# A decode kernel's down weights: twelve rows per partition by one load in halves, and 16 partitions of 16 rows by four short loads

## The chip, the cores and the metric

The kernel runs on one core of a Trainium2 chip. The metric is device time in microseconds (us) for one execution. Several executions are timed; a profile is taken from one more. The profile's span goes from the first to the last instruction of that execution, and the execution's own time is a little longer than its span.

## The reference

Two parts are computed from small activations (8 rows of 512) and large weights and caches, and then combined. The window W is 2048 positions.

```
xn = layernorm(x)                                  # [8, 1, 512]
q  = xn @ wq                                       # 32 heads of 128
k, v = the last W positions of the caches          # 8 KV heads, each serves 4 query heads
o  = softmax(q k^T * 128**-0.5) v
s  = o @ wo                                        # [8, 1, 512]

h  = sigmoid(xn @ w_gate) * (xn @ w_up)            # [8, 1, 1792]
g  = silu(h @ w_down)                              # [8, 1, 512]

out = x + s * g
```

All inputs are bf16. w_down has 1792 rows of 512 numbers, 1 KB each. K and V of the window are 64 MiB together; all weights are about 13 MiB.

## The kernel before

**Tiles and slots.** Everything large is loaded by SP's DMA queue (`q0`, nc.sync) into nine slots of 16 KB per partition (pool `slots`, list `empty`, line 85). A wish for a load is put on the list `todo`; `pump()` (line 87) issues wishes in their order as long as a slot is free, and `free()` (line 92) gives a slot back and pumps again. So the order of the loads is the order in which they are wished for, lines 171 to 192: gate weights, up weights, down weights, the short loads ("sides") among the query weights, then K tiles and, three behind them, V tiles of each batch and half, then the output weights `wo` in four pieces of 16, 10, 4 and 2 rows per partition.

**How SP waits.** Each load raises one of eight DMA semaphores in turn; a load waits until the load eight places before it has landed. It also waits for the engine that must have read the old contents of its slot, for K and V tiles PE. The first load of all, x, goes through ACT's queue and takes the first semaphore.

**A load's engines.** A load of 128 partitions is worked on by all 16 DMA engines of the core, each of which has its own list of packets. The short loads have 5, 3 or 9 partitions.

**The down weights.** 1792 rows are 14 for each of 128 partitions; they are cut in three. `want_down` (line 143) loads the first 1408 rows as 11 consecutive rows for each of 128 partitions (tile `wd_sb`). The remaining 384 rows go into a tile `side` (lines 122 to 141): 240 rows as 15 rows on 16 partitions by two loads of five and two of three partitions (`LOW`, `SF`), and 144 rows as 4 rows on 36 partitions from partition 32 on by four loads of nine (`MID`, `SM`, `M_AT`). Each of these loads takes every fourth partition. The first 32 partitions of the tile are zeroed by POOL first (line 126), because some of them stay unfilled and are read as zero weights.

**What is done with them.** h is made from gate and up products (lines 273 to 306). It must be turned so that its 1792 numbers lie on partitions like the rows of w_down. For the first 1408 numbers PE transposes strided views of `h_bf` directly. For the side rows POOL first copies h into `h_side` in the order of the side partitions (lines 309 to 323; zeroed on line 249), and PE transposes that. DVE and ACT copy the turned h to `hT_sb` (lines 331 to 333). After the query products (lines 347 to 362), 26 products with `wd_sb` and `side` accumulate `d_ps` (lines 363 to 375). The gate value g is finished on lines 395 to 401.

**The rest.** For each batch PE transposes K tiles (line 456; DVE copies them out on line 461), multiplies them with q (line 474), ACT makes exponentials (line 494), PE turns those (line 563) and multiplies with V (line 584). At the end PE multiplies with `wo` (line 706) as its four pieces land, DVE combines and four small transfers write the output (lines 717 to 724).

Of the kernel before, what the change touches and what calls it, by code (L numbers as in the profile page):

```python
# [10 lines left out]
def kernel(  # L11
# [13 lines left out]
    nc = tc.nc  # L25
    P = 128
    B, _, D = A_x.shape
# [4 lines left out]
    F = B_w_gate.shape[1]  # L32
    KT = D // P
# [14 lines left out]
    bf16 = mybir.dt.bfloat16  # L48
# [12 lines left out]
    work = ctx.enter_context(tc.tile_pool(name="work", bufs=1))  # L61
# [17 lines left out]
    q0, q1 = nc.sync, nc.scalar  # L79
    k_tiles = {}  # L80
    v_tiles = {}
    weights = {}
# [10 lines left out]
        empty.append(int(t[1][4:]))  # L93
        pump()

    def want_rows(name, w, per, r0, r1, step=None):
        def f(tag):
            t = slots.tile([P, r1 - r0, w.shape[1]], bf16, name=name, tag=tag)
            for a in range(r0, r1, step or r1 - r0):
                z = a + (step or r1 - r0)  # L100
                q0.dma_start(
                    out=t[:, a - r0 : z - r0, :],
                    in_=w.rearrange("(p r) n -> p r n", r=per)[:, a:z, :],
                )
            rows_of[(name, r0)] = (t, tag)
            for r in range(r0, r1):
                weights[(name, r)] = t[:, r - r0, :]

        todo.append((True, f))

    LOW, SF = (5, 5, 3, 3), 15
    MID, SM = 9, 4
    SP = 4 * max(LOW)
    M_AT = 32
    MP = 4 * MID
    MT = 11
    m0 = MT * P
    m1 = m0 + SF * sum(LOW)
    assert m1 + SM * MP == F
    side = {}  # L120

    def want_side(w, q, at, count, rows, base, of):
        def f(tag=None):
            if tag:
                t = slots.tile([P, SF, w.shape[1]], bf16, name="side", tag=tag)
                nc.gpsimd.memzero(t[:M_AT])  # L126
                side["t"] = t
                rows_of[("side", 0)] = (t, tag)
                for r in range(SF):
                    weights[("wd_sb", MT + r)] = t[: M_AT + MP if r < SM else SP, r]  # L130
            q0.dma_start(  # L131
                out=side["t"][at + q : at + q + 4 * (count - 1) + 1 : 4, :rows].rearrange(
                    "p s n -> p (s n)"
                ),
                in_=w[base : base + of * count * rows, :].rearrange(
                    "(p q s) n -> q p (s n)", q=of, s=rows
                )[q % of],
            )

        todo.append((not side, f))  # L140
        side["asked"] = True

    def want_down(w):
        def f(tag):
            t = slots.tile([P, MT, w.shape[1]], bf16, name="wd_sb", tag=tag)
            q0.dma_start(
                out=t[:].rearrange("p t n -> p (t n)"),
                in_=w[: MT * P, :].rearrange("(p t) n -> p (t n)", t=MT),
            )
            rows_of[("wd_sb", 0)] = (t, tag)  # L150
            for r in range(MT):
                weights[("wd_sb", r)] = t[:, r, :]

        todo.append((True, f))
# [13 lines left out]

    RT = 32
    Z = 32  # L170
    want_rows("wg_sb", B_w_gate, KT, 0, KT, 2)
    want_rows("wu_sb", B_w_up, KT, 0, KT, 2)
    want_down(B_w_down)
    sides = []
    for q in range(4):
        sides.append((q, 0, LOW[q], SF, m0 + q // 2 * 2 * LOW[0] * SF, 2))
        sides.append((q, M_AT, MID, SM, m1, 4))
    for x in sides[:2]:
        want_side(B_w_down, *x)
    for i in range(2):  # L180
        want_rows("wq_sb", A_wq, KT, 2 * i, 2 * i + 2)
        for x in sides[2 + 3 * i : 5 + 3 * i]:
            want_side(B_w_down, *x)
    order = [(b, i) for b in range(B) for i in range(NQ)]
    AHEAD = 3
    for n in range(len(order) + AHEAD):
# [4 lines left out]
    for t0, t1 in ((0, 16), (16, 26), (26, 30), (30, RT)):  # L191
# [15 lines left out]
        out=perm[:].rearrange("k (l p) -> k l p", l=G),  # L207
        in_=ident[:].rearrange("k (p l) -> k l p", l=G),
# [11 lines left out]
        out=rstd[:], in_=mv[:, 1:2], func=AF.Sqrt, bias=eps_t[:], scale=1.0  # L220
# [4 lines left out]
        out=xn_bf[:],  # L225
# [8 lines left out]
    for kt in range(KT):  # L234
        nc.tensor.transpose(  # L235
            out=xnT_ps[:, kt, :],
            in_=xn_bf[:].rearrange("b (p kt) -> b kt p", kt=KT)[:, kt, :],
# [5 lines left out]

    hT_sb = work.tile([P, MT + SF, Z], bf16, name="hT_sb")
    nc.gpsimd.memzero(hT_sb[:])  # L245
    oP_sb = work.tile([P, RT, Z], bf16, name="oP_sb")
    nc.gpsimd.memzero(oP_sb[:])
    h_side = work.tile([B, SF, M_AT + MP], bf16, name="h_side")
    nc.gpsimd.memzero(h_side[:])

    NB = D // P

# [10 lines left out]
    with nc.allow_low_precision(reason="zeros and a one"):  # L263
        nc.vector.reduce_sum(
            out=band[:], in_=ident[:].rearrange("k (q t) -> k q t", t=RT), axis=AX.X
        )
        nc.vector.reduce_sum(
            out=pick[:], in_=ident[:].rearrange("k (q t) -> k t q", t=RT), axis=AX.X
# [21 lines left out]
    h_bf = ktpool.tile([P, CU * P], bf16, name="h_bf", tag="kT")  # L290
    for k in range(F // FC):
        u_ps = ps_t.tile([B, FC], f32, name="u_ps", tag="t")
        for kt in range(KT):
# [8 lines left out]
            out=h_bf[:B, k * FC : (k + 1) * FC],  # L302
# [3 lines left out]
        )  # L306
    free(rows_of[("wu_sb", 0)])
    hT_ps = ps_m.tile([P, MT + SF, B], bf16, name="hT_ps", tag="m")
    for h in range(2):
        c = LOW[2 * h]  # L310
        at = m0 + h * 2 * LOW[0] * SF
        nc.gpsimd.tensor_copy(
            out=h_side[:, :, : 4 * c].rearrange("b t (e q) -> b t e q", q=4)[
                :, :, :, 2 * h : 2 * h + 2
            ],
            in_=h_bf[:B, at : at + 2 * c * SF].rearrange(
                "b (e q t) -> b t e q", q=2, t=SF
            ),
        )
    nc.gpsimd.tensor_copy(  # L320
        out=h_side[:, :SM, M_AT:],
        in_=h_bf[:B, m1:F].rearrange("b (p t) -> b t p", t=SM),
    )
    cuts = [h_bf[:B, :m0].rearrange("b (p t) -> b t p", t=MT)[:, t] for t in range(MT)]
    rows = [P] * MT + [M_AT + MP] * SM + [SP] * (SF - SM)
    cuts += [h_side[:, t, : rows[MT + t]] for t in range(SF)]
    for t, x in enumerate(cuts):
        nc.tensor.transpose(
            out=hT_ps[: rows[t], t, :], in_=x, identity=ident[:B, :B]
        )  # L330
    nc.vector.tensor_copy(out=hT_sb[:, :MT, :B], in_=hT_ps[:, :MT])
    for k, t0, t1 in ((M_AT + MP, MT, MT + SM), (SP, MT + SM, MT + SF)):
        nc.scalar.copy(out=hT_sb[:k, t0:t1, :B], in_=hT_ps[:k, t0:t1])

    def fold(out_ps, src, start, stop):
        for j in range(NB):
# [38 lines left out]
    for e in range(2):  # L375
# [3 lines left out]
        for r in range(rep):  # L379
            nc.tensor.transpose(  # L380
                out=qT_ps[:, r].rearrange("p g z -> p (g z)"),
                in_=q_bf[:, r * Dh : (r + 1) * Dh],
# [3 lines left out]
            out=qm_sb[:, :, G * e : G * (e + 1), M0 : M0 + rep].rearrange(  # L386
                "p b g r -> p r g b"
            ),
            in_=qT_ps[:, :, :, :B],
# [14 lines left out]
    for j in range(NB):  # L404
# [15 lines left out]
        out=turn_rows[:].rearrange("k (x l r) -> k x l r", x=NU, l=G),  # L420
        in_=ident[:].rearrange("k (l x r) -> k x l r", x=NU, l=G),
    )
    sel_e = consts.tile([P, 2, Hq], f32, name="sel_e")
    for e in range(2):
        nc.vector.reduce_sum(
            out=sel_e[:, e, :].rearrange("k (i h) -> k i h", i=NQ),
            in_=ident_f[:].rearrange(
                "k (i m e h) -> k e i h m", i=NQ, m=NJ // 2, e=2
            )[:, e],
# [290 lines left out]
    for j in range(NB):  # L720
        (q0, q1)[j % 2].dma_start(
            out=out.flatten_outer_dims()[:, j * P : (j + 1) * P],
            in_=y_bf[Z * j : Z * j + B, :],
# [31 lines left out]
```

## Time and profile before

| what | us |
|---|---|
| median of 3 runs (199.06 to 199.09) | 199.06 |
| the profiled execution | 199.33 |
| its span | 197.5 |
| PE busy | 157.4 |
| DVE busy | 125.4 |
| ACT busy | 40.7 |
| POOL busy | 11.0 |

The mean granted clock of PE over the span is 0.965 of full speed. The span holds 4796 instructions. DMA moved 81.32 MB, 412 GB/s over the span. Busy time is summed over the span for each engine; the engines run side by side, so the rows do not add up to the span. An engine's share says little by itself: what a change is worth is read where it acts, from what is waited for there.

### The profile page before, as it was taken

To read this page: it belongs to the slowest core of one execution; us is meant where nothing else is said; L and a number is where in the kernel's file an instruction comes from. 1 tells how busy PE (TensorE), PEld (TensorE's weight loads), DVE (VectorE), ACT (ScalarE), POOL (GpSimd) and SP (SyncE) were. 2 spreads that over 40 slices of the span, in tenths; PEclk is the share of its full clock that TensorE was granted. 3 is DMA by queue.
4 is the path that set the end of the run, shared out by engine and by line. 5 is a ranking of instruction groups with operands and counts; after the bars stand their busy time and mean duration, and the time that the engine had idled before them with its cause. 6 is when DMAs were issued, how large, how long until landed. Compare 5 with 4: busy or idle time off the path is not lost.

```text
span 197.5 us, 4796 instructions
## 1 busy us (share of the span) xinstructions
PE 157.4 (80%) x2112; PEld 103.1 (52%) x2112; DVE 125.4 (63%) x245; ACT 40.7 (21%) x95; POOL 11.0 (6%) x22
## 2 busy tenths in 40 slices
PE   0089559999788898799979987999799979976733
PEld 0034325776664565466545654566466556655531
DVE  4623106999797696679666965796669658935201
ACT  0522022006306001600160016001600160071000
POOL 8910200000000000000000000000000000000000
PEclk9999859999999999999999999999999999999975
DMA  6999999999999999999999999999999999999980
GB/s 205 424 440 435 431 434 435 425 425 431 423 425 425 438 428 435 431 425 428 422 433 431 435 425 433 428 418 428 428 438 431 428 428 431 428 423 425 428 366 21
DMA packets 6396, 81.32 MB, mean 412 GB/s; under 512 B 812, under 2 KB 820, under 8 KB 1624
## 3 DMA queue, kind: packets, MB, share of 16 engines
q1 hardware_dynamic: 6328, 81.01, 96.6%
q8 instruction: 16, 0.26, 0.5%
q10 hardware_dynamic: 48, 0.01, 0.0%
q14 instruction: 4, 0.03, 0.0%
HBM read 81.01 MB, written 0.01 MB: 410 GB/s over the span
## 4 chain that ended last, share of the span: by engine, by line
DMA 73%; PE 22%; POOL 3%; SPq 0%; issue 0%; DVE 0%; POOLq 0%
DMA v_sb<-in_A_v_cache_dram 46%; DMA wo_sb<-in_A_wo_dram 14%; PE kT_ps L456 11%; DMA wq_sb<-in_A_wq_dram 7%; DMA k_sb<-in_A_k_cache_dram 6%; PE o_ps L584 4%; PE s_ps L474 3%; POOL side L126 2%; PE m_ps L614 1%; PE fin_ps L706 1%; PE pT_ps L563 1%; SPq L131 0%; POOL perm L206 0%; POOL hT_sb L245 0%; DVE prod L717 0%
## 5 line engine op out<-in xcount | busy, mean ns | idle before, releaser
L461 DVE COPY kT_sb<-kT_ps 128x1024 bf16<-128x1024 bf16 x128 | 84.2, 683 | 28.9 <-PE kT_ps L456 25.0
L456 PE MATMUL kT_ps<-perm,k_sb 128*128 128x128 bf16 x1024 | 72.6, 220 | 3.7 <-DMA k_sb<-in_A_k_cache_dram 3.7
L456 PEld LDWEIGHTS <-k_sb 128*128 128x128 bf16 x1024 | 58.8, 98 | 26.1 <-issue 16.8
L584 PE MATMUL o_ps<-v_sb,pT_sb 128*32 128x256 bf16 (+1 forms) x352 | 36.5, 327 | 9.0 <-DMA v_sb<-in_A_v_cache_dram 7.6
L474 PE MATMUL s_ps<-kT_sb,qm_sb 128*32 128x512 bf16 x256 | 25.6, 389 | 1.3 <-DVE kT_sb L461 1.1
L494 ACT ACTIVATE p_buf<-s_ps,st 32x512 bf16<-32x512 f32 x32 | 21.7, 679 | 15.4 <-DVE st L487 15.1
L584 PEld LDWEIGHTS <-pT_sb 128*32 128x32 bf16 (+1 forms) x352 | 12.3, 101 | 21.7 <-issue 19.7
L604 ACT ACTIVATE o_sb<-o_ps,fac 128x512 f32<-128x512 f32 (+1 forms) x8 | 4.9, 608 | 60.9 <-PE o_ps L584 60.9
L568 DVE COPY pT_sb<-pT_ps 128x1024 bf16<-128x1024 bf16 x16 | 10.8, 676 | 1.8 <-PE pT_ps L563 1.8
L474 PEld LDWEIGHTS <-qm_sb 128*32 128x32 bf16 x256 | 7.0, 93 | 8.0 <-issue 1.3
L563 PE MATMUL pT_ps<-turn_rows,p_buf 128*128 128x128 bf16 x128 | 10.7, 227 | 0.0
L563 PEld LDWEIGHTS <-p_buf 128*128 128x128 bf16 x128 | 9.4, 149 | 0.2 <-issue 0.2
L521 ACT ACTIVATE w_row<-w 1x128 f32<-1x128 f32 x8 | 2.5, 309 | 30.6 <-DVE w L514 30.6
L235 PE MATMUL xnT_ps<-ident,xn_bf 8*128 8x8 bf16 x4 | 0.3, 176 | 10.6 <-DVE xn_bf L224 10.6
L385 DVE COPY qm_sb<-qT_ps 128x128 bf16<-128x128 bf16 x2 | 1.4, 881 | 8.7 <-PE qT_ps L380 8.7
L301 DVE TENSOR_TENSOR h_bf<-sig,u_ps 8x448 bf16<-8x448 f32 x4 | 2.4, 608 | 6.6 <-PE u_ps L294 6.1
L278 PE MATMUL g_ps<-wg_sb,xnT_sb 128*8 128x448 bf16 x16 | 5.7, 544 | 0.3 <-DVE xnT_sb L242 0.3
L494 ACT ACTIVATION_READ_ACCUMULATOR p_buf<-s_ps,st 32x1 f32 x32 | 5.9, 184 | 0.0
L706 PE MATMUL fin_ps<-wo_sb,oP_sb 128*32 128x128 bf16 x128 | 3.3, 263 | 3.1 <-DMA wo_sb<-in_A_wo_dram 3.1
L487 DVE TENSOR_REDUCE st<-s_ps 128x1 f32<-128x512 f32 x8 | 5.4, 681 | 0.5 <-PE s_ps L474 0.5
L235 PEld LDWEIGHTS <-xn_bf 8*128 8x128 bf16 x4 | 0.2, 117 | 10.6 <-DVE xn_bf L224 10.6
L352 PE MATMUL q_ps<-wq_sb,xnT_sb 128*32 128x512 bf16 x32 | 3.1, 526 | 3.2 <-DMA wq_sb<-in_A_wq_dram 3.2
(88 smaller groups left out, 92.0 us busy)
## 6 DMA issues: line engine op xcount, KB each, us to landing
k_sb<-in_A_k_cache_dram SPq DMA_DIRECT2D x16, 2048.0 KB
v_sb<-in_A_v_cache_dram SPq DMA_DIRECT2D x16, 2048.0 KB
wq_sb<-in_A_wq_dram SPq DMA_DIRECT2D x2, 2048.0 KB
wo_sb<-in_A_wo_dram SPq DMA_DIRECT2D x1, 2048.0 KB
wg_sb<-in_B_w_gate_dram SPq DMA_DIRECT2D x2, 896.0 KB
wu_sb<-in_B_w_up_dram SPq DMA_DIRECT2D x2, 896.0 KB
wd_sb<-in_B_w_down_dram SPq DMA_DIRECT2D x1, 1408.0 KB
wo_sb<-in_A_wo_dram SPq DMA_DIRECT2D x1, 1280.0 KB
```

Of the source, the lines that this page charges most:

```text
L126: nc.gpsimd.memzero(t[:M_AT])
L278: nc.tensor.matmul(g_ps[:], lhsT=xnT_sb[:, kt, :B], rhs=weights[("wg_sb", kt)][:, k * FC : (k + 1) * FC], start=(kt == 0), stop=(kt == KT ...
L456: nc.tensor.transpose(out=kT_ps[:, c, :], in_=k_sb[:, j * CU + h * CH + c, :], identity=perm[:],)
L461: nc.vector.tensor_copy(out=kT[(b, u)][:, h * CH : (h + 1) * CH, :], in_=kT_ps[:])
L474: nc.tensor.matmul(s_ps[b][NR * l : NR * (l + 1), :], lhsT=qm_sb[:, b, i * G + l, o : o + Z], rhs=t[:, :, PG * l : PG * (l + 1)], start=(u ...
L487: nc.vector.tensor_reduce(out=st[b][:], in_=s_ps[b][:], axis=AX.X, op=ALU.max, negate=True)
L494: nc.scalar.activation(out=p_buf[b % 2][rows, :, l, :], in_=s[rows, :].rearrange("k (c p) -> k p c", p=PG), func=AF.Exp, bias=st[b][rows, ...
L563: nc.tensor.transpose(out=pT_ps[:, c, :], in_=p_buf[b % 2][:, :, :, h * CH + c].rearrange("k p l -> k (p l)"), identity=turn_rows[:],)
L568: nc.vector.tensor_copy(out=pT[b][:, h * CH : (h + 1) * CH, :], in_=pT_ps[:])
L584: nc.tensor.matmul(o_ps[r] if b < WIDE else o_ps[r, 0:2], lhsT=pT[b][:, c, r], rhs=x, start=(c == 0), stop=(c == CU - 1), tile_position=(0 ...
L604: nc.scalar.activation(out=o[:, :n], in_=o_ps[:, :n], func=AF.Copy, scale=fac.pop(b)[:])
L706: nc.tensor.matmul(fin_ps[Z * j : Z * (j + 1), :], lhsT=oP_sb[:, t, :], rhs=weights[("wo_sb", t)][:, j * P : (j + 1) * P], start=(t == 0), ...
```

## The change

The 1792 rows are cut in two instead of three. The large load takes 12 rows for each of 128 partitions (1536 rows). The remaining 256 rows go to 16 partitions, 16 rows each, by two loads of five partitions and two of three; each takes every second partition. There are no loads of nine partitions. All 16 partitions of the side tile are filled, so nothing is zeroed, and the side rows of h lie in an order that PE can transpose from `h_bf` directly, so `h_side`, its zeroing and POOL's three copies go. There are 28 instead of 26 transposes and products.

Some loads are issued as two halves of 64 partitions each: the first of the two gate loads, the large down load, and both query loads. The gate and up loads are two each of two rows per partition, as before. The number of loads on SP's queue ahead of the first K tile is 15 before and after. All four short loads now stand ahead of the last query load: two of five partitions between the large load and the first query load, two of three between the query loads.

```diff
+    def halves(parts, out, in_):
+        n = P // parts
+        for a in range(0, P, n):
+            q0.dma_start(out=out[a : a + n], in_=in_[a : a + n])
+
-    def want_rows(name, w, per, r0, r1, step=None):
+    def want_rows(name, w, per, r0, r1, parts=(1,)):
         def f(tag):
             t = slots.tile([P, r1 - r0, w.shape[1]], bf16, name=name, tag=tag)
-            for a in range(r0, r1, step or r1 - r0):
-                z = a + (step or r1 - r0)
-                q0.dma_start(
-                    out=t[:, a - r0 : z - r0, :],
-                    in_=w.rearrange("(p r) n -> p r n", r=per)[:, a:z, :],
+            n = (r1 - r0) // len(parts)
+            for a, k in zip(range(r0, r1, n), parts):
+                halves(
+                    k,
+                    t[:, a - r0 : a - r0 + n, :],
+                    w.rearrange("(p r) n -> p r n", r=per)[:, a : a + n, :],
                 )
...
-    LOW, SF = (5, 5, 3, 3), 15
-    MID, SM = 9, 4
-    SP = 4 * max(LOW)
-    M_AT = 32
-    MP = 4 * MID
-    MT = 11
+    LOW, SF = (5, 5, 3, 3), 16
+    SP = sum(LOW)
+    MT = 12
     m0 = MT * P
-    m1 = m0 + SF * sum(LOW)
-    assert m1 + SM * MP == F
+    assert m0 + SF * SP == F
     side = {}
 
-    def want_side(w, q, at, count, rows, base, of):
+    def want_side(w, p0, q, count):
         def f(tag=None):
             if tag:
                 t = slots.tile([P, SF, w.shape[1]], bf16, name="side", tag=tag)
-                nc.gpsimd.memzero(t[:M_AT])
...
+            at = m0 + p0 * SF
             q0.dma_start(
-                out=side["t"][at + q : at + q + 4 * (count - 1) + 1 : 4, :rows].rearrange(
-                    "p s n -> p (s n)"
-                ),
-                in_=w[base : base + of * count * rows, :].rearrange(
-                    "(p q s) n -> q p (s n)", q=of, s=rows
-                )[q % of],
+                out=side["t"][p0 + q : p0 + 2 * count : 2].rearrange("p s n -> p (s n)"),
+                in_=w[at : at + 2 * count * SF, :].rearrange(
+                    "(p q s) n -> q p (s n)", q=2, s=SF
+                )[q],
             )
...
             t = slots.tile([P, MT, w.shape[1]], bf16, name="wd_sb", tag=tag)
-            q0.dma_start(
-                out=t[:].rearrange("p t n -> p (t n)"),
-                in_=w[: MT * P, :].rearrange("(p t) n -> p (t n)", t=MT),
+            halves(
+                2,
+                t[:].rearrange("p t n -> p (t n)"),
+                w[: MT * P, :].rearrange("(p t) n -> p (t n)", t=MT),
             )
...
-    want_rows("wg_sb", B_w_gate, KT, 0, KT, 2)
-    want_rows("wu_sb", B_w_up, KT, 0, KT, 2)
+    want_rows("wg_sb", B_w_gate, KT, 0, KT, (2, 1))
+    want_rows("wu_sb", B_w_up, KT, 0, KT, (1, 1))
     want_down(B_w_down)
...
     for i in range(2):
-        want_rows("wq_sb", A_wq, KT, 2 * i, 2 * i + 2)
-        for x in sides[2 + 3 * i : 5 + 3 * i]:
-            want_side(B_w_down, *x)
+        for q in range(2):
+            want_side(B_w_down, i * 2 * LOW[0], q, LOW[2 * i])
+        want_rows("wq_sb", A_wq, KT, 2 * i, 2 * i + 2, (2,))
...
-    h_side = work.tile([B, SF, M_AT + MP], bf16, name="h_side")
-    nc.gpsimd.memzero(h_side[:])
...
-    rows = [P] * MT + [M_AT + MP] * SM + [SP] * (SF - SM)
-    cuts += [h_side[:, t, : rows[MT + t]] for t in range(SF)]
+    cuts += [h_bf[:B, m0:F].rearrange("b (p t) -> b t p", t=SF)[:, t] for t in range(SF)]
+    rows = [P] * MT + [SP] * SF
...
-    for k, t0, t1 in ((M_AT + MP, MT, MT + SM), (SP, MT + SM, MT + SF)):
-        nc.scalar.copy(out=hT_sb[:k, t0:t1, :B], in_=hT_ps[:k, t0:t1])
+    nc.scalar.copy(out=hT_sb[:SP, MT:, :B], in_=hT_ps[:SP, MT:])
```

More of the change, by code (lines that the diff above doesn't have):

```diff
@@ L129, in f @@
                 for r in range(SF):
-                    weights[("wd_sb", MT + r)] = t[: M_AT + MP if r < SM else SP, r]
+                    weights[("wd_sb", MT + r)] = t[:SP, r]
+            at = m0 + p0 * SF
             q0.dma_start(
-                out=side["t"][at + q : at + q + 4 * (count - 1) + 1 : 4, :rows].rearrange(
-                    "p s n -> p (s n)"
-                ),
-                in_=w[base : base + of * count * rows, :].rearrange(
-                    "(p q s) n -> q p (s n)", q=of, s=rows
-                )[q % of],
+                out=side["t"][p0 + q : p0 + 2 * count : 2].rearrange("p s n -> p (s n)"),
+                in_=w[at : at + 2 * count * SF, :].rearrange(
+                    "(p q s) n -> q p (s n)", q=2, s=SF
+                )[q],
             )
@@ L170 @@
     Z = 32
-    want_rows("wg_sb", B_w_gate, KT, 0, KT, 2)
-    want_rows("wu_sb", B_w_up, KT, 0, KT, 2)
+    want_rows("wg_sb", B_w_gate, KT, 0, KT, (2, 1))
+    want_rows("wu_sb", B_w_up, KT, 0, KT, (1, 1))
     want_down(B_w_down)
[L174 to L178, printed above, removed]
-        want_side(B_w_down, *x)
     for i in range(2):
-        want_rows("wq_sb", A_wq, KT, 2 * i, 2 * i + 2)
-        for x in sides[2 + 3 * i : 5 + 3 * i]:
-            want_side(B_w_down, *x)
+        for q in range(2):
+            want_side(B_w_down, i * 2 * LOW[0], q, LOW[2 * i])
+        want_rows("wq_sb", A_wq, KT, 2 * i, 2 * i + 2, (2,))
     order = [(b, i) for b in range(B) for i in range(NQ)]
@@ L308 @@
     hT_ps = ps_m.tile([P, MT + SF, B], bf16, name="hT_ps", tag="m")
[L309 to L323, printed above, removed]
     cuts = [h_bf[:B, :m0].rearrange("b (p t) -> b t p", t=MT)[:, t] for t in range(MT)]
-    rows = [P] * MT + [M_AT + MP] * SM + [SP] * (SF - SM)
-    cuts += [h_side[:, t, : rows[MT + t]] for t in range(SF)]
+    cuts += [h_bf[:B, m0:F].rearrange("b (p t) -> b t p", t=SF)[:, t] for t in range(SF)]
+    rows = [P] * MT + [SP] * SF
     for t, x in enumerate(cuts):
```

## The prediction

> **What bounds the kernel now.** I read the page's slices first (its second part), then the DMA queues, the chain that ended last, and then windows of the span's two ends.
>
> ```profile
> DMA  6999999999999999999999999999999999999980
> GB/s 205 424 440 435 431 434 435 425 425 431 423 425 425 438 428 435 431 425 428 422 433 431 435 425 433 428 418 428 428 438 431 428 428 431 428 423 425 428 366 21
> ...
> q1 hardware_dynamic: 6328, 81.01, 96.6%
> q8 instruction: 16, 0.26, 0.5%
> ...
> DMA 73%; PE 22%; POOL 3%; SPq 0%; issue 0%; DVE 0%; POOLq 0%
> ```
>
> The sixteen DMA engines are busy in every slice but the two ends, at about 430 GB/s. All weights and caches, 81.01 MB, go through SP's one queue. The chain is DMA for 73%, and its PE pieces lie beside transfers that were running anyway. So the end comes when the queue is empty, plus a tail.
>
> ```profile
> 189.50:190.00 0.50, 0.39 (x28) 0.24 (x17) 0.00 (x0) 0.00 (x0) 0.00 (x0) 1.00 1.11 467
> 190.00:190.50 0.50, 0.00 (x0) 0.00 (x0) 0.00 (x0) 0.00 (x0) 0.00 (x0) 0.77 0.82 344
> 190.50:191.00 0.50, 0.00 (x0) 0.00 (x0) 0.00 (x0) 0.00 (x0) 0.00 (x0) 0.50 0.71 295
> 191.00:191.50 0.50, 0.00 (x0) 0.00 (x0) 0.00 (x0) 0.00 (x0) 0.00 (x0) 0.50 0.80 324
> 191.50:192.00 0.50, 0.14 (x8) 0.14 (x11) 0.00 (x0) 0.00 (x0) 0.00 (x0) 0.50 0.92 360
> 192.00:192.50 0.50, 0.50 (x28) 0.50 (x24) 0.00 (x0) 0.00 (x0) 0.00 (x0) 0.50 0.67 262
> 192.50:193.00 0.50, 0.50 (x24) 0.42 (x16) 0.00 (x0) 0.00 (x0) 0.00 (x0) 0.50 0.45 172
> 193.00:193.50 0.50, 0.50 (x23) 0.40 (x16) 0.00 (x0) 0.00 (x0) 0.00 (x0) 0.50 0.07 25
> ```
>
> Columns: window, length, busy time of PE, PEld, DVE, ACT and POOL, PE's clock, DMA share, GB/s. The rate does not drop at once; it thins out over 3.5 us. The engines do not finish together, and the output waits for the last one. Each engine works through a list of its own, so what counts is not the sum of bytes but the list of the slowest engine. This is the view on which the forecast rests.
>
> The trace's records of single packets and of completion counts give those lists. A load of all partitions is counted complete by 16 engines, one of nine partitions by nine, one of five by five, one of three by three. A 16384-byte packet takes 611 ns and the next one on its engine starts 607 ns after it, so 27.0 GB/s for each engine. The first K load, right behind the weights, completes on its sixteen engines at 29.56 to 29.98 us (eight), 30.28 to 30.52 (three), 31.06 and 31.14, and 32.39 to 32.45 (three): those that carried the short loads are late in that order. From there I followed each engine packet by packet. The sixteen instruction blocks of q8 come to eight engines in turn, at 31.8 us, 41.1 and so on, and each delays its engine by about 1.42 us (881 ns for itself, 1158 instead of 611 for the next packet, less 14 of overlap and the 4 by which packets overlap). None comes to the five engines that carry the five-row and three-row loads, which is why those can carry more.
>
> **The change, part by part.** *Bytes per engine.* The large load gives every engine 8 rows of 11 KB now (88 KB) and 8 of 12 KB then (96). The short loads give now: to the first three engines 4 x 15 + 4 x 4 = 76 KB, the next two 2 x 15 + 16 = 46, the next four 16, the last seven nothing. Then: 4 x 16 = 64, 2 x 16 = 32, nothing, nothing. Sums 164, 134, 104, 88 before; 160, 128, 96, 96 after. At 607 ns for 16 KB this is -0.15, -0.23, -0.30 and +0.30 us. The last data of the slowest engine of each group ends, by my tracking, at 193.22, 193.04, 193.36 and 193.02. After: 193.07, 192.81, 193.06 and 193.32. The last one ends at 193.32 in place of 193.36: **-0.04 us**. The gain of one group is the loss of another. (Of the four engines with 16 KB more, one can't be told apart from the last seven; if the 193.02 is its, the next is 192.95 and the sum is -0.11.)
>
> *Halves of 64 partitions.* One gate load, the large load and both query loads are halved. The count of loads on SP stays 15: four halves more, four short loads fewer. All sixteen engines serve a half too, with four packets each where a whole load has eight. No load of before goes to 64 partitions. Lower bound: nothing. The nearest row is the short load of five: five engines write 15360 bytes each to partitions of one 20-partition stretch and take 573 ns, 26.8 GB/s, the rate of any other. Upper bound, if half the partitions took only half the rate: the halves hold 0.92 + 1.57 + 4.19 = 6.68 MB, 15.5 us at 432 GB/s, so 15.5 us more. I take nothing, because the row with the fewest partitions shows no loss, though its partitions lie four apart; the upper bound is the first rival.
>
> *Start.* Before:
>
> ```profile
> 1.00:2.00 1.00, 0.00 (x0) 0.00 (x0) 0.00 (x0) 0.00 (x0) 0.90 (x4) 1.00 0.62 79
> 2.00:3.00 1.00, 0.00 (x0) 0.00 (x0) 0.26 (x1) 0.00 (x0) 1.00 (x1) 1.00 0.63 173
> 3.00:4.00 1.00, 0.00 (x0) 0.00 (x0) 1.00 (x1) 0.00 (x0) 1.00 (x1) 1.00 0.91 366
> 4.00:5.00 1.00, 0.00 (x0) 0.00 (x0) 1.00 (x1) 0.00 (x0) 1.00 (x1) 1.00 0.98 409
> ```
>
> The first weight packet starts at 1.77 us. By 5.0 us 432 GB/s would have moved 1395 KB, and 1027 KB were moved: 0.85 us lost. A first load of half the size may gain some of it, 0.85 at most, or lose as much where its four packets run out before the next half is described. Each first packet took 560 to 1412 ns where later ones of 7168 bytes take 272, whatever load stood behind it, so I take 0, with 0.2 either way.
>
> *SP and POOL.*
>
> ```profile
> L131 SPq DMA_DIRECT2D side<-in_B_w_down_dram x8: 690/744/864, 5.1 to 16.9; - x8
> L126 POOL MEMSET side<- x1: 3287/3287/3287, 1.8 to 1.8; 32x3840 uint32 x1
> ```
> ```profile
> SPq L131 <- POOL hT_sb L245: 2.2, 1, 2.2
> ```
>
> The zeroing of the side tile (3.29 us of POOL) and SP's wait for POOL go, with POOL's second zeroing (0.51) and three copies (0.73 + 0.30). Worth nothing: the load in front of the wait, the large one, lands only at 15.35 us, 10 us after SP goes on, so the queue was full. Behind SP's wait stood the short loads and the query loads, and nobody waits for those before 22 us. Four short issues of 744 ns become four of about 413 (a gate load's), 1.3 us less on SP. SP's later waits are for the eighth load before; every place of that chain moves earlier or stays, since the number of loads is the same.
>
> *PE.* Two transposes and two products more (26 to 28 tiles), 0.11 us for each product (1.64 us by 15). What moves is the second query half: all short loads now lie ahead of it. The first three engines have 160 KB of down weights in front of it, not 88 + 53 = 141, so it lands 0.7 us later than 26.67. From there PE's row of work runs 5.5 us to 32.2; then it would end near 33.1, and the first K load, landed by 32.3, waits 0.6 us longer than the 0.04 of before. The cover is PE's own waiting: it sat 1.24 us at 81.09 for a V load, and the page gives PE 7.6 us of waits for V and 3.7 for K. Without that cover 0.6 us would be lost. SP's K and V issues that follow wait for PE to free a slot, but run some 33 us ahead of their landing at 42.57 us, so 0.6 us starves no engine. ACT's one copy for two, and DVE's 96 columns for 88, lie beside the wait for the query load.
>
> *Tail.* Unchanged: from the last completion, 193.69 us, to the end of the span at 197.5.
>
> Sum: span 197.5 - 0.04; the profiled execution is 199.33, so 199.29. The median of the runs is 199.06, 0.27 below the profiled one: 199.02. Several engines of three groups now stand within 0.3 us of the last, and a new start reorders them by up to 0.2, which raises the largest more than it lowers it: I add 0.1 and say **199.1 us**.
>
> **Rivals.** *Halves are slow (slower).* If two engines that write into the same half of the partitions share a way in, the eight halves (6.68 MB) run at down to half rate, and everything behind them in the queue is late by up to 15.5 us: 206 to 214.6. For it: no load of before has this form, and before's short loads are placed four partitions apart, so they can't show the crowding. Against it: 573 ns for five engines in 20 partitions. It decides from a loss of 2.6% in those 15.5 us, 0.4 us. [...]
>
> *An instruction block falls on a loaded engine (slower).* The last of the sixteen blocks starts at 191.889 us on an engine whose data ended at 191.887. PE has eight more instructions, and eight engines take the blocks in turn. If the block, or one more, comes to an engine that still has data, that engine ends 1.42 us later; on one that ends at 193.3 the end moves by up to 1.4: 199.5 to 200.5, deciding from 0.4. Against it: that engine's data now end 0.30 us earlier, at 191.59, and the block's time follows PE, which follows the loads.
>
> *A better start (faster).* The 0.85 us lost before 5 us come back in part with a smaller first load: 198.2 to 198.6. Against it: the slow first packets are slow on every engine.
>
> **How the numbers follow.** About 0.2%, 0.4 us, can be told from no change. No change, 198.7 to 199.45: 0.52. Halves slow: 0.19, kept that high because no row excludes it. Instruction block: 0.16. Better start: 0.13. So faster 0.13, same 0.52, slower 0.35. The range is 198.5 to 200.6; what lies outside is mostly the first rival, about 0.2. The forecast's own range is 198.7 to 199.45.
>
> **What would show it.** Right: packets of halved loads at 26 to 27 GB/s, 416 GB/s or more in the windows from 5 to 19 us, the thin end again 3 us or so wide with the last completion within 0.3 us of 193.7, and one POOL zeroing less with no time from it. PE's first K transposes start near 33.1. Wrong: windows near 215 to 350 GB/s while the gate, large or query halves run (first rival), a q8 packet after 185 us with data still behind it (second), over 1200 KB by 5 us (third). If PE no longer waits for the V load near 81 us, my cover was gone.

## The result and the profile after

The changed kernel takes 221.25 us (median of 6, 220.2 to 221.87) beside 199.08 us of the kernel before: a ratio of 1.1106, 95% interval 1.1075 to 1.1137. The forecast was 199.1 us with a range of 198.5 to 200.6, so it was wrong by 22 us. What came is the first rival, "Halves are slow", and more than the 15.5 us of its upper bound.

The profiled execution of the changed kernel took 221.87 us, its span 220.1. The page's slices, DMA queues and chain, after:

```profile
PEclk9999555555699999999999999999999999999985
DMA  6999999999999999999999999999999999999980
GB/s 150 358 317 225 208 220 140 194 179 426 423 426 429 424 429 432 429 429 432 426 435 426 435 426 433 429 432 424 429 426 432 429 429 426 432 426 427 433 349 9
...
q1 hardware_dynamic: 6320, 81.01, 96.6%
q8 instruction: 16, 0.26, 0.4%
...
DMA 74%; PE 23%; SPq 1%; issue 0%; DVE 0%
```

The same bytes go through the same queue, the chain is DMA as before, and from the tenth slice (49.5 us) on the rate is the old one. All the loss lies in the first nine slices, at 140 to 358 GB/s where before they had 205 to 440. The line of digits does not show it: the engines are "9" busy there too. A busy engine here is one with a packet under way, not one that moves bytes at its rate: at 23 us, in a window below, the share is 0.97 at 197 GB/s. Only the GB/s line tells the two apart. (PEclk, PE's granted clock, is 0.50 from 22 to 59 us; the K loads run at 442 GB/s at the same 0.50, in the window at 52 us below, so it is not what holds the queue.)

Windows of the changed kernel (window, length, busy time of PE, PEld, DVE, ACT, POOL, PE's clock, DMA share, GB/s):

```profile
7.00:8.00 1.00, 0.00 (x0) 0.00 (x0) 0.53 (x2) 0.35 (x1) 0.00 (x0) 1.00 0.99 401
15.00:16.00 1.00, 1.00 (x7) 0.49 (x6) 0.00 (x0) 0.61 (x2) 0.00 (x0) 1.00 0.97 197
23.00:24.00 1.00, 0.00 (x0) 0.00 (x0) 0.00 (x0) 0.00 (x0) 0.00 (x0) 0.50 0.97 197
33.00:34.00 1.00, 0.06 (x4) 0.06 (x8) 0.00 (x0) 0.00 (x0) 0.00 (x0) 0.50 1.06 115
34.00:35.00 1.00, 1.00 (x12) 0.41 (x16) 0.00 (x0) 0.00 (x0) 0.00 (x0) 0.50 1.40 147
35.00:36.00 1.00, 0.84 (x8) 0.00 (x0) 0.00 (x0) 0.00 (x0) 0.00 (x0) 0.50 0.25 33
36.00:37.00 1.00, 0.00 (x0) 0.00 (x0) 0.00 (x0) 0.00 (x0) 0.00 (x0) 0.50 1.25 197
43.00:44.00 1.00, 0.00 (x0) 0.00 (x0) 0.00 (x0) 0.00 (x0) 0.00 (x0) 0.50 1.15 164
52.00:53.00 1.00, 1.00 (x16) 0.41 (x12) 0.00 (x0) 0.61 (x2) 0.00 (x0) 0.50 1.03 442
```

The kernel before, same columns, in two of these places:

```profile
15.00:16.00 1.00, 1.00 (x5) 0.33 (x3) 0.00 (x0) 0.20 (x1) 0.00 (x0) 1.00 1.07 455
23.00:24.00 1.00, 0.51 (x8) 0.04 (x1) 0.00 (x0) 0.00 (x0) 0.00 (x0) 0.51 1.03 442
```

At 7 us the whole gate and up loads run at 401 GB/s. At 15 us the halves of the large load are on their way: 197 in place of 455. At 23 us it is the first query half: 197. Around 35 and 43 us it is worse than half. A window counts a packet whole where it starts, so with packets longer than the window neighbours must be read together: the 33 GB/s and the DMA share of 0.25 at 35 us belong to the 1.40 before them, and the four windows from 33 to 37 us have 123 GB/s on average. At 52 us the first whole K load runs at 442.

The trace's packet records say the same for single packets. A 16384-byte packet took 611 ns in the kernel before; in the changed kernel the median is 1244 ns from 23 to 31 us, 2472 from 33 to 36, 1749 from 42 to 47, and 611 again from 51. The completion counts say where the time went: the last data of the queue are in at 216.29 us in place of 193.69, 22.60 later, and the span is 22.6 longer. What follows the last data takes 3.81 us in both (spans are printed to 0.1 us). PE only passes it on; its waits for query weights, before and after (us in total, times, longest):

```profile
PE q_ps L352 <- DMA wq_sb<-in_A_wq_dram: 3.2, 1, 3.2
```
```profile
PE q_ps L329 <- DMA wq_sb<-in_A_wq_dram: 27.7, 2, 15.0
```

### The profile page after: what moved, and what is told of

Same layout as the page of the kernel before. It is cut to its first block, busy times and chain, and to the rows that moved or that the text cites. A ratio compares the mean times of both kernels' runs of the same rounds, so it can differ in the third digit from the quotient of the medians.

```text
span 220.1 us, 4795 instructions
## 1 busy us (share of the span) xinstructions
PE 159.4 (72%) x2116; PEld 104.2 (47%) x2116; DVE 125.6 (57%) x245; ACT 40.7 (18%) x94; POOL 6.1 (3%) x17
## 4 chain that ended last, share of the span: by engine, by line
DMA 74%; PE 23%; SPq 1%; issue 0%; DVE 0%
DMA v_sb<-in_A_v_cache_dram 40%; DMA wq_sb<-in_A_wq_dram 13%; DMA wo_sb<-in_A_wo_dram 13%; PE kT_ps L433 10%; DMA wd_sb<-in_B_w_down_dram 8%; PE o_ps L561 3%; PE s_ps L451 3%; PE d_ps L343 1%; SPq L99 1%; PE m_ps L591 1%; PE fin_ps L683 1%; PE pT_ps L540 1%; PE q_ps L329 1%; PE qT_ps L357 0%; PE b_ps L314 0%
## 5 line engine op out<-in xcount | busy, mean ns | idle before, releaser
L433 PE MATMUL kT_ps<-perm,k_sb 128*128 128x128 bf16 x1024 | 73.4, 221 | 2.4 <-DMA k_sb<-in_A_k_cache_dram 2.4
L433 PEld LDWEIGHTS <-k_sb 128*128 128x128 bf16 x1024 | 59.6, 99 | 24.5 <-issue 17.4
L329 PE MATMUL q_ps<-wq_sb,xnT_sb 128*32 128x512 bf16 x32 | 3.8, 628 | 27.7 <-DMA wq_sb<-in_A_wq_dram 27.7
L329 PEld LDWEIGHTS <-xnT_sb 128*32 128x32 bf16 x32 | 0.9, 129 | 29.8 <-DMA wq_sb<-in_A_wq_dram 28.7
L354 ACT ACTIVATE q_bf<-q_ps 128x512 bf16<-128x512 f32 x2 | 1.1, 594 | 30.6 <-PE q_ps L329 30.6
L208 DVE CAST x_f<-x_bf 8x512 f32<-8x512 bf16 x1 | 4.5, 4452 | 2.2 <-DMA x_bf<-in_A_x_dram 2.2
```

The source lines that it names most:

```text
L208: nc.vector.tensor_copy(out=x_f[:], in_=x_bf[:])
L329: nc.tensor.matmul(q_ps[e][Z * g : Z * (g + 1), :], lhsT=xnT_sb[:, kt, :], rhs=weights[("wq_sb", kt)][:, c0 : c0 + D], start=(kt == 0), st ...
L433: nc.tensor.transpose(out=kT_ps[:, c, :], in_=k_sb[:, j * CU + h * CH + c, :], identity=perm[:],)
```

## The experiments

Two readings had to be told apart: the loads of 64 neighbouring partitions are slow, or the short loads, which now go to every second partition in place of every fourth, are. Behind that stood the question why the loss exceeds 15.5 us. "The last data" is the last completion in the queue, 193.69 us in the kernel before. Runs without an interval are single executions, and the last data are always those of the one profiled execution. They depend on the slowest engine of that execution: e8 and e11 give every engine the same bytes and differ by 0.76 us.

| run | us | ratio to before, 95% | last data |
|---|---|---|---|
| changed kernel | 221.25 | 1.1106 (1.1075 to 1.1137) | 216.29 |
| e1_rows_s2 | 202.7 | 1.0192 (1.0162 to 1.0222) | 197.32 |
| e2_halves_s4 | 219.98 | 1.1037 (1.1021 to 1.1053) | 215.24 |
| e3_rows_s4 | 200.42 | 1.0052 (1.0034 to 1.007) | 194.61 |
| e4_parity_s4 | 200.91 | 1.0084 (1.0071 to 1.0097) | 195.35 |
| e5_quarters_s4 | 220.44 | | 214.89 |
| e6_sbuf_halves | 220.04 | | 214.49 |
| e7_dram_halves | 200.69 | | 195.09 |
| e8_whole_s4 | 199.8 | 1.0039 (1.0025 to 1.0053) | 193.61 |
| e9_halves_sides_last | 214.76 | 1.0779 (1.0761 to 1.0797) | 209.09 |
| e10_rows_s1 | 203.32 | 1.0207 (1.0191 to 1.0222) | 197.64 |
| e11_whole_15 | 200.12 | 1.0051 (1.0037 to 1.0064) | 194.37 |

**e1: the same loads cut in two along the row.** All 128 partitions, half of each row: as many loads, of the same bytes.

```diff
-        n = P // parts
-        for a in range(0, P, n):
-            q0.dma_start(out=out[a : a + n], in_=in_[a : a + n])
+        n = out.shape[1] // parts
+        for a in range(0, out.shape[1], n):
+            q0.dma_start(out=out[:, a : a + n], in_=in_[:, a : a + n])
```

> The changed kernel with its eight halves cut along the row instead of along the partitions: the same number, order and bytes of loads, each to 128 partitions; the short loads stay two partitions apart. Theory A (a load that reaches only 64 neighbouring partitions runs at half rate, and that is the whole loss): 199.1 us. Theory B (the halves cost 15.5 us and the short loads, crowded two apart, the other 6.5): 205.5 us. Theory C (a load with only four packets per engine or with half the bytes is slow wherever it goes): about 214 to 221 us, as the bytes per load are the same.

It took 202.7 us (202.44 to 204.35). 18.6 of the 22.2 us are gone with this one edit, but not all. That excludes C and lies between A and B.

**e2 and e3: the short loads four partitions apart, with halves (e2) and with e1's rows (e3).** This brings back `h_side`, its zeroing and POOL's copies.

```diff
-    SP = sum(LOW)
+    SP = 4 * max(LOW)
...
-                out=side["t"][p0 + q : p0 + 2 * count : 2].rearrange("p s n -> p (s n)"),
+                out=side["t"][p0 // LOW[0] + q :: 4][:count].rearrange("p s n -> p (s n)"),
```

> The changed kernel with its halves of 64 partitions kept, and the short loads put four partitions apart, as before the change (with the zeroing and the two copies that this needs). Theory A: 221, the placement of the short loads is nothing. Theory B: 214.6 us, the 15.5 us of the halves alone. A third reading, that the extra 6.5 us comes from engines that fall out of step while halves run, whatever the short loads' places: 221.

> Both undone: halves cut along the row, short loads four partitions apart. What is left of the change is twelve rows for eleven, and no loads of nine partitions. By the prediction's sum of bytes per engine 199.0 us (-0.04); if the nine-partition loads were worth keeping, 199.3 or more; if the loss were anything else in the change, over 200.

e2 took 219.98 us, e3 200.42 (12 runs, 199.26 to 201.09). e3 is over 200, so by its expectation something else costs time too; e8 takes that up. So the step from two to four partitions is worth 1.3 us with halves and 2.3 without, and with the short loads four apart the halves cost 19.6 us. One window of e1, the same of e3:

```profile
17.00:18.00 1.00, 1.00 (x7) 0.43 (x5) 0.45 (x1) 0.26 (x1) 0.00 (x0) 1.00 0.78 221
```
```profile
17.00:18.00 1.00, 1.00 (x7) 0.43 (x5) 0.47 (x1) 0.24 (x1) 0.00 (x0) 1.00 0.99 418
```

Right behind the short loads of five, the rate of e1 falls to 221 GB/s; e3 stays at 418. Behind the short loads of three it falls once more, to 303 and 279 GB/s in the two windows from 24 to 26 us, where e3 has 451 and 426.

**e4: halves of every second partition.** 64 partitions again, with the same number of bytes in each and the same count of loads as e2, but spread over all 128.

```diff
-        n = P // parts
-        for a in range(0, P, n):
-            q0.dma_start(out=out[a : a + n], in_=in_[a : a + n])
+        for a in range(parts):
+            q0.dma_start(out=out[a::parts], in_=in_[a::parts])
```

> As e2_halves_s4, but a half is every second partition of all 128 instead of 64 neighbours: same bytes, packets and number of loads. If it is which partitions a load reaches that matters: 199 to 203 us (some engines may still meet on neighbouring partitions). If it is that a load reaches 64 partitions at all, or has four packets per engine: the time of e2_halves_s4, 214 to 221 us.

It took 200.91 us, 19.1 less than e2. Not the number of partitions is dear here, but which.

**e5: quarters of 32 neighbouring partitions.** As e2, each half cut once more, eight loads more.

```diff
-        n = P // parts
+        n = P // (2 * parts if parts > 1 else 1)
```

> As e2_halves_s4 with each half cut once more into two loads of 32 neighbouring partitions (eight loads more, so SP's eight semaphores come out as before). If a stretch of 32 reaches as many ways into the memory as one of 64: 218 to 222 us, no more than e2_halves_s4. If the rate goes with the number of partitions (a quarter of 128, a quarter of the rate): 15.5 to 31 us more than that, 235 to 251 us.

220.44 us beside e2's 219.98: 32 neighbours at a time cost what 64 do. Had the rate gone with the number of partitions, a quarter of it for a quarter of 128, quarters would have lost another 15.5 us or more (an estimate from 6.68 MB at 432 GB/s). Why 32 cost what 64 cost, no run shows.

**e6 and e7: which side decides.** Each takes the neighbours on one side only: e6 writes 64 neighbouring partitions from every second partition's rows in DRAM, e7 the other way round.

```diff
-        for a in range(0, P, n):
-            q0.dma_start(out=out[a : a + n], in_=in_[a : a + n])
+        for a in range(parts):
+            q0.dma_start(out=out[a * n : a * n + n], in_=in_[a :: parts])      # e6
+            q0.dma_start(out=out[a :: parts], in_=in_[a * n : a * n + n])      # e7
```

> Which end of the transfer crowds: as e2_halves_s4, but a half writes 64 neighbouring partitions and reads every second partition's rows in DRAM, the rows that e4_parity_s4 reads. The weights of the halved loads so lie on other partitions than the products take them from, and the output is not the reference's; bytes, packets and order are those of e2_halves_s4. If the written partitions decide: 220 us, as e2_halves_s4. If the read rows decide: 201 us, as e4_parity_s4.

> The mirror of e6_sbuf_halves: every second partition is written and 64 neighbouring partitions' rows are read; again the halved weights lie on other partitions than the products take them from. If the written partitions decide: 201 us. If the read rows decide: 220 us.

220.04 and 200.69 us. The slices of e6, then those of e7:

```profile
GB/s 147 361 314 227 180 210 201 195 198 423 426 432 426 428 432 429 432 429 429 429 432 429 425 426 429 423 431 423 432 426 432 429 432 429 429 423 428 428 388 51
```
```profile
GB/s 191 368 431 442 422 435 425 428 432 435 428 420 425 435 428 432 428 425 432 428 432 427 432 425 432 427 425 435 432 425 425 432 432 428 432 427 425 426 334 13
```

The partitions written decide: e6 is 0.06 us from e2 and e7 0.22 from e4, whichever rows in DRAM are read.

**e8: nothing cut.** The split into twelve rows and 16 partitions of 16 rows alone, with the short loads four apart.

```diff
-                2,
+                1,
...
-    want_rows("wg_sb", B_w_gate, KT, 0, KT, (2, 1))
+    want_rows("wg_sb", B_w_gate, KT, 0, KT, (1, 1))
...
-        want_rows("wq_sb", A_wq, KT, 2 * i, 2 * i + 2, (2,))
+        want_rows("wq_sb", A_wq, KT, 2 * i, 2 * i + 2)
```

> e3_rows_s4 with nothing cut: the gate load in two of two rows, the large load and both query loads whole, so eleven loads in place of fifteen and packets as long as before. If e3's 1.2 us over the kernel before come from its shorter packets (32 more for each engine at some 5 ns, 0.16 us) and from its start, this is nearer: 199.0 to 199.6, as the prediction's sum of bytes has it (-0.04). If they come from the missing nine-partition loads or from the twelve rows: 200.4 again. If SP's eight semaphores, which now stand four places off, matter: over 200.4.

199.8 us, between its expectations, and its last data are in at 193.61, 0.08 before those of the kernel before. So this execution shows no loss in the queue from the new spread of bytes; e11, of the same spread, has its last data 0.68 later than the kernel before, so the 0.08 are finer than such a comparison can tell. What e8 loses, it loses behind the last data: 4.29 us from there to the end of the span in place of 3.81 (e11).

**e9: e2 with the four short loads behind both query loads.** Same loads, other order, so that no engine carries more than another while halves run.

```diff
-        for q in range(2):
-            want_side(B_w_down, i * 2 * LOW[0], q, LOW[2 * i])
         want_rows("wq_sb", A_wq, KT, 2 * i, 2 * i + 2, (2,))
+    for i in range(2):
+        for q in range(2):
+            want_side(B_w_down, i * 2 * LOW[0], q, LOW[2 * i])
```

> e2_halves_s4 with the four short loads behind both query loads instead of among them. e2 lost 19.6 us against e3_rows_s4, 4 us more than the 15.5 that 6.68 MB at half rate make. If these 4 us come from five engines that the short loads put behind, which still write halves while the others are on the K load: with the short loads last all engines leave the halves together, 215 to 216.5 us. If the halves cost 19.6 by themselves: 220.

214.76 us, 5.2 less than e2. Its last data are in at 209.09, 15.48 behind e8's 193.61: about the 15.5 us of half rate. That it fits to the tenth is luck. e8 has fewer loads and no halved first load; against e3 and e4, which have e9's count of loads but the short loads among the query halves, the same difference is 14.48 and 13.74 us. Windows of e9:

```profile
15.00:16.00 1.00, 1.00 (x8) 0.44 (x6) 0.00 (x0) 0.72 (x2) 0.00 (x0) 1.00 0.97 197
31.00:32.00 1.00, 0.73 (x8) 0.29 (x12) 0.00 (x0) 0.00 (x0) 0.00 (x0) 0.50 0.95 197
35.00:36.00 1.00, 0.00 (x0) 0.00 (x0) 0.00 (x0) 0.00 (x0) 0.00 (x0) 0.50 1.10 246
43.00:44.00 1.00, 1.00 (x12) 0.16 (x4) 0.00 (x0) 0.77 (x2) 0.00 (x0) 0.50 1.03 442
```

From 33 to 37 us the changed kernel moved 123 GB/s on average, e9 205. The four query halves' first and last completions among the 16 engines, in us:

| half | e9 | e2 |
|---|---|---|
| 1 | 25.75 to 26.32 | 26.78 to 30.10 |
| 2 | 30.67 to 31.23 | 31.67 to 35.08 |
| 3 | 35.59 to 36.16 | 36.79 to 42.41 |
| 4 | 40.52 to 41.06 | 41.80 to 49.66 |

In e9 the engines stay within 0.6 us of each other and each half takes 4.92 us. In e2 the five engines that carry short loads are 3.3 us late at the first half and 7.9 at the fourth. The others run into the next half. In the changed kernel five engines end the second query half 1.8 to 2.5 us behind the others' last at 31.36 and the third at 39.96 to 43.38, behind 38.31; its packets of 2472 ns between the two are four times 611, those of 1244 twice. That the short loads' place among the halves makes the 5.2 us is shown by the order alone. That it does so through the lag is read from the completions. That two engines, and then four, take turns is my estimate from these multiples of 611; no run shows it, and the packet records do not name the engine.

**e10: e1 with the short loads on neighbouring partitions.**

```diff
-                out=side["t"][p0 + q : p0 + 2 * count : 2].rearrange("p s n -> p (s n)"),
+                out=side["t"][p0 + q * count : p0 + (q + 1) * count].rearrange("p s n -> p (s n)"),
...
-                    "(p q s) n -> q p (s n)", q=2, s=SF
+                    "(q p s) n -> q p (s n)", q=2, s=SF
```

> e1_rows_s2 (no halves of partitions) with the short loads on neighbouring partitions instead of every second one. Four apart gave 200.4, two apart 202.7. If what counts is how many engines of a short load write into the same group of four partitions (five engines in two groups now, three groups at two apart, five at four apart), this is slower than two apart: 205 to 210 us. If the placement's price was in the permutation or the zeroing of the side tile and not in the partitions: 202.7.

203.32 us, between the two expectations and 0.6 above e1. Against e3 (four apart) the three steps stand at 200.42, 202.7 and 203.32; e1's four runs spread from 202.44 to 204.35, so the last step is not clear of noise. The ten packets of 16 KB of the two loads of five took 611 ns each in e3. In e1 they begin at 611 and the last three took 1208 to 1246; in e10 they begin at 611 and the last five took 1632 to 1899. That is about two and three times 611, what two and three engines taking turns would give, an estimate from the 611 alone; which engines met where was not shown. The total does not grow in that measure; why stays open.

**e11: where e8's time went.** e8 has 11 loads ahead of the first K tile, the kernel before 15. SP ends by waiting for its eight semaphores in a row; the count of loads sets which of them the last outputs raise (in the kernel before the fifth to eighth, at 196.04, 196.23, 196.43 and 196.62 us). e11 is e8 with each short load as two of eight rows: 15 loads.

```diff
-            q0.dma_start(
-                out=side["t"][p0 // LOW[0] + q :: 4][:count].rearrange("p s n -> p (s n)"),
+            for r in range(0, SF, SF // 2):
+                q0.dma_start(
+                    out=side["t"][p0 // LOW[0] + q :: 4][:count, r : r + SF // 2],
...
```

> Nothing is halved; each of the four short loads (every fourth partition) goes as two of eight rows, so 15 loads stand ahead of the first K tile as in the kernel before, in place of 11. Theory S (the 0.7 us of the version with nothing halved come from SP's closing waits: the number of loads sets which of SP's eight semaphores is raised last, and SP's last five waits ended 0.5 us behind the last output there): SP's closing waits fall between the output's completions again, span 197.4 to 197.6, time 199.0 to 199.3. Theory B (the 0.7 us come from the new spread of bytes over the engines): the spread is the same, so 199.7 to 200.0.

200.12 us, a miss for both by its time, but the tail tells. SP's closing waits (us in total, times, longest), of the kernel before, e8 and e11:

```profile
SPq L750 <- DMA out_dram<-y_bf: 0.7, 3, 0.4
```
```profile
SPq L742 <- DMA out_dram<-y_bf: 0.9, 1, 0.9
```
```profile
SPq L743 <- DMA out_dram<-y_bf: 0.9, 4, 0.4
```

With 15 loads SP sees the outputs land one after another; with 11 it sits in one wait of 0.9 us and does the others after it. From the last data to the end of the span it is 3.81 us before, 4.29 in e8, 3.73 in e11, and 3.69 to 3.81 in every other run, of 15 loads or 23 (the same place among eight). The completion counts say the same: from the last output's landing to the end of the span it is 0.83 us before and in e11, and 1.40 in e8. So the 0.5 us in e8's tail are the count's. (The medians of e8 and the kernel before differ by 0.7 us, their profiled executions by 0.4, 199.72 and 199.33.) But e11's last data came at 194.37, 0.76 behind e8's: two engines end behind the others, at 194.16 and 194.37 where the next is at 193.58. One of them falls behind at about 140 us: the load landing there is in at 140.01 on fifteen engines and at 141.06 on the last, 2 us after an instruction block of q8 at 139.06. e8 has a block at the same place, at 138.92 us, and no engine behind it: its load there ends at 139.54 and 139.60 on the last two. That looks like the second rival, a block on a loaded engine; no run was made for it, and it stays argued.

No version beat the kernel before.

## Why the prediction was wrong

**The step that failed** is "Halves of 64 partitions", where I wrote "I take nothing, because the row with the fewest partitions shows no loss". The row was the 573 ns of the five-partition load, with partitions four apart. The lower bound was taken where the upper bound was right: e9's last data came 15.48 us after e8's (13.7 and 14.5 after e4's and e3's), where the sum had 0 and the bound 15.5. The prediction itself said that such a row "can't show the crowding", and then let it decide, with 0.81 on the side without loss. A row that cannot show an effect is no evidence against it. The half rate of the upper bound was an estimate that no row of before showed; e9's query halves moved 1.049 MB in 4.92 us, 213 GB/s, 0.49 of the sum's 432. That engines share a way in, the condition of the first rival, was not shown by any run; what the runs show is the rate and the partitions it goes with.

**The bound was too low**, because it priced the halves alone. Two terms were missing from the sum:

| term | forecast | measured | from |
|---|---|---|---|
| twelve rows, no nines (last data) | -0.04 | -0.08 | e8 |
| halves, engines in step | 0 (bound 15.5) | +15.5 | e9 to e8, last data |
| short loads among the halves | not priced | +5.2 | e2 to e9 |
| short loads two apart, not four | not priced | +1.3 | changed kernel to e2 |

Together 21.9 of 22.2 us. The rows are steps of one chain of runs from the kernel before to the changed one, so that they add up proves nothing of its own; each row is as good as its one pair of runs. The short loads were counted in bytes per engine; their move from every fourth to every second partition stood in the diff and was not costed at all.

**Bytes per engine** held as far as single executions can tell: -0.08 (e8) for -0.04. That the two agree so closely is luck: e11 has the same bytes per engine and +0.68.

**Start.** The third rival was wrong in sign. The changed kernel's windows from 1 to 5 us:

```profile
1.00:2.00 1.00, 0.00 (x0) 0.00 (x0) 0.00 (x0) 0.00 (x0) 0.89 (x4) 1.00 0.03 8
2.00:3.00 1.00, 0.00 (x0) 0.00 (x0) 0.81 (x1) 0.00 (x0) 1.00 (x4) 1.00 0.96 179
3.00:4.00 1.00, 0.00 (x0) 0.00 (x0) 1.00 (x1) 0.00 (x0) 1.00 (x1) 1.00 1.07 294
4.00:5.00 1.00, 0.00 (x0) 0.00 (x0) 1.00 (x1) 0.00 (x0) 1.00 (x2) 1.00 0.99 229
```

710 KB by 5 us, not over 1200, and fewer than the 1027 of before: the first gate load is a half too. With halves of every second partition, slices 1 and 2 are still short (191 and 368 in e7, for 205 and 424 before), and e3, whose first load is halved along the row, moved 1033 KB by 5 us, so a halved first load gave nothing back in any form. This and what else keeps e3, e4 and e7 0.6 to 1.1 us above e8 was not taken apart.

**SP and POOL.** No run speaks against it, and none tests it alone: e2 brings POOL's work back and is 1.3 us shorter, but it moves the short loads too.

**PE.** e8 shows the step without the flood of halves. The lines of its timeline (start, us, operation, count, idle time before and its releaser):

```profile
27.24 1.90 PE L344 MATMUL q_ps<-wq_sb,xnT_sb 128*32 128x512 bf16 x16 [4.36 <-DMA wq_sb<-in_A_wq_dram]
...
30.35 1.89 PE L358 MATMUL d_ps<-side,hT_sb 20*32 20x512 bf16 x16
...
33.95 1.35 PE L448 MATMUL kT_ps<-perm,k_sb 128*128 128x128 bf16 x11
```

The second query load is used from 27.24 us, 0.6 behind the 26.67 of before (0.7 forecast), the first K transposes start at 33.95, 0.85 later than the 33.1 forecast (why was not taken apart), and the last data are not late. The cover was there: PE still waits 6.6 us for V loads and 2.4 for K, where it waited 7.6 and 3.7.

**Tail** held: 3.81 us before and after. The thin end, too, is of the old form; the changed kernel's windows:

```profile
212.50:213.00 0.50, 0.00 (x0) 0.00 (x0) 0.00 (x0) 0.00 (x0) 0.00 (x0) 0.87 0.76 307
213.50:214.00 0.50, 0.00 (x0) 0.00 (x0) 0.00 (x0) 0.00 (x0) 0.00 (x0) 0.50 0.66 266
214.50:215.00 0.50, 0.50 (x24) 0.50 (x27) 0.00 (x0) 0.00 (x0) 0.00 (x0) 0.50 0.15 57
215.50:216.00 0.50, 0.49 (x21) 0.30 (x16) 0.00 (x0) 0.00 (x0) 0.00 (x0) 0.50 0.05 20
```

One engine alone ends at 216.29, the next two at 215.07 and 215.06. The last instruction block, at 213.07, did not make that 1.2 us: from the load that ends at 138.53 us on, the last engine is 1.2 to 1.3 us behind the next. What put it there was not separated; it is small beside the rest.

## What to carry to other kernels

Ask of a load not how many partitions it writes but which: cut along the row (e3, 200.42 us), or take every second partition (e4, 200.91), and no neighbouring half goes alone (e2, 219.98). Where loads of few partitions lie between large ones, spread them four apart (1.3 us less than two apart with halves, 2.3 without) and keep them away from any load that is already crowded: the four short loads hold 0.26 MB, 0.6 us at 432 GB/s, and their place among the halves cost 5.2. And when a bound is large and no row of the trace can show the effect, weigh it by the bound and not by the nearest row that looks harmless.

## What the runs showed of the hardware that was not expected

- Loads that write 64 neighbouring partitions move 213 GB/s (e9), loads of 32 cost no more in total (e5, 220.44 us beside 219.98), while 64 partitions at every second place run at the full rate (425 to 447 GB/s in e4's third to sixth slices). The rows read make no such difference (e6, 220.04 us for e2's 219.98; e7, 200.69 for e4's 200.91).
- DMA engines show as fully busy meanwhile (a share of 0.97 at 197 GB/s at 23 us of the changed kernel): packets stretch, from 611 to 1244 ns and, with the engines out of step, to 2472.
- Short loads two partitions apart cost the other engines too: 244 and 221 GB/s in the windows from 16 to 18 us (e1) for 408 and 418 with four apart (e3). Five of sixteen engines at a standstill would still leave some 284 (an estimate from e3's rate).
- The number of loads ahead of the first K tile moved the end by 0.5 us: from the last data to the span's end it is 4.29 us with 11 of them (e8), and 3.69 to 3.81 with 15 or 23, which stand at the same place among the queue's eight semaphores.
